# Attention in front of two dense layers: first pairs of heads without DRAM, chunks split at 128, K's high part on ScalarE

## The chip, the cores and the metric

The kernel runs on one core of a Trainium2 chip. The metric is the device time of one execution in microseconds; lower is better. The core has a matrix engine (TensorE, PE in the profile, with its weight loads as a row of their own, PEld), VectorE (DVE), ScalarE (ACT), GpSimd (POOL) and a sync engine (SP) from whose queue all DMA transfers are issued here. Every engine works through its own instructions in the order in which they stand in the program.

## What is computed

Attention over 4 batches of 8 heads, 576 positions of 64 values, with a bias from running sums of `s`, and then two dense layers with a nonlinearity each:

```python
def _attn_ref(q, k, v, s):
    scale = 1.0 / np.sqrt(D)
    scores = scale * np.matmul(q, k.transpose(0, 1, 3, 2))
    causal = np.triu(np.ones((S, S), dtype=bool), k=1)
    s_pos = np.maximum(s, 0.0)
    cum = np.cumsum(s_pos, axis=-1)
    bias = -(cum[:, :, :, None] - cum[:, :, None, :])
    scores = np.where(causal, -1000000000.0, scores + np.minimum(bias, 0.0))
    scores = scores - np.max(scores, axis=-1, keepdims=True)
    attn = np.exp(scores)
    attn = attn / (np.sum(attn, axis=-1, keepdims=True) + 1e-09)
    return np.matmul(attn, v)
x = attn_out.transpose(0, 2, 1, 3).reshape(2304, 512)
h = x @ w_in;  x = (h - np.tanh(h)) @ w_out
h = x @ w_in2; x = (h * np.clip(h + 3.0, 0.0, 6.0) / 6.0) @ w_out2
```

## The kernel before

A planner, `Plan`, holds every step with its engine, a duration, its predecessors and buffers and a priority (`PRIO`), and fixes the order on each engine before the program is built. All products of the attention but the last one, and of the dense layers, take numbers split into a high part that TensorE's faster float format holds exactly and a low part.

The 32 heads are worked on in 16 pairs (`heads(p)`). Of a pair, q and k come in transposed (64 rows by 2 x 576, tile `tq`). Four copies are made of them: Q high and K high (`q1` on ACT, `kh` on DVE) in the tiles Q and K of `firsts` (four sets), and in the tiles of `seconds` (two sets) once more Q high (`q2`, a DMA from tile to tile) and K high (`k2`, on ACT) with the low parts (`ql`, `kl`: subtractions on POOL). Rows 64 to 67 of Q and K carry the bias: two rows of K hold the running sums, as high and low part, and two rows of Q the negated maxima.

The running sums are made once, on DVE, at the start (L369 to L374, function `cum`): clipping, a scan, two copies. They go to DRAM (`cdram`) and from there into K by one DMA for each pair; for the first head they go from tile to tile by DMA (L256, K<-rb).

Softmax needs the row maxima before the scores. For each head PE makes the scores a first time from the high parts (L479, lists `MAXT`: five row blocks of up to 128 rows take 384, 576, 512, 256 and 128 columns, in one tile `wide` of two banks and two single banks), and DVE takes each block's maximum under the causal mask (L488), straight from the banks. The maxima of a pair are split and turned on DVE (L513 to L517), written to DRAM (`mo`, mdram) and read back as rows of Q (`mi`, Q<-mdram).

Then come the scores proper, transposed, in four chunks of columns (L572, lists `CHUNKS`): for each chunk one product from `seconds`, one from `firsts`, and one with `maskT` and the identity that adds the causal mask. The weights of these products are blocks of 128 columns of K. ACT takes the exponential (L575) and PE multiplies with v (L603) in plain float32, two passes for each product, into two banks that split the 576 queries at 256; ACT copies the two banks out (L626). Sums and results go on by DMA.

From about 200 us on the two dense layers follow on PE (L828, L859, then L1120, L1196); their weights are split on ACT and DVE during the attention and after. In the planner's rules PE steps that follow each other have a latency of 0.30 us between them.

## Time and profile before

| what | value |
|---|---|
| time, median of 3 runs | 969.19 us (969.17 to 972.99) |
| the profiled execution's own time | 968.87 us |
| its span, first to last instruction | 967.1 us |
| PE busy | 946.1 us (98%) |
| PE busy from 50 to 300 us | 249.5 us of 250 |
| DVE, ACT, POOL busy | 670.0, 467.9, 160.7 us |
| chain that ended last | PE 94%, DVE 3%, ACT 1%, DMA 1% |

How to read it: busy time is the time in which an engine had an instruction running. Matmuls are pipelined, so one matmul's listed duration overlaps the next one's, and a stretch in which PE is busy throughout can still hold fewer matmuls than another one: the number of matmuls in a window tells more than the busy share. Weight loads (PEld) run beside the matmul in front of them. The profiled execution is 0.3 us from the median.

### The profile page before, as it was taken

What the parts mean: (1) busy time and instruction counts of PE and PEld (TensorE: products, weight loads), DVE (VectorE), ACT (ScalarE), POOL (GpSimd) and SP (SyncE); (2) the same over time, 40 slices, a digit from 0 to 9 for tenths busy, and PEclk for the clock granted to TensorE, in tenths of its full rate; (3) what the DMA queues carried; (4) which work ended last, traced back from release to release, by engine and by line L of the source; (5) the groups of instructions that cost most, each with busy time, mean ns of one, the idle gap of its engine ahead of it and who ended that gap; (6) DMA issues with size and microseconds to landing.
All of it is one profiled execution on the core that took longest, in us unless ns stands there. A gap on an engine that the chain in (4) does not pass through costs nothing.

```text
span 967.1 us, 14956 instructions
## 1 busy us (share of the span) xinstructions
PE 946.1 (98%) x5560; PEld 838.7 (87%) x5560; DVE 670.0 (69%) x1107; ACT 467.9 (48%) x714; POOL 160.7 (17%) x106
## 2 busy tenths in 40 slices
PE   3999999999999999999999999999999999999998
PEld 3777777778878888998888888999999999999998
DVE  7887777759998667767766835555775567765763
ACT  2677667755444433444443433444454434544442
POOL 8344646520000000003322223000000000000000
PEclk9999999999999999999999999999999999999999
DMA  4656776676635356556455690765696657866562
GB/s 123 183 164 175 214 184 196 166 237 261 188 94 191 151 217 224 176 180 226 160 209 186 213 316 31 256 218 201 241 324 220 235 201 248 317 219 235 201 225 98
DMA packets 70521, 195.91 MB, mean 203 GB/s; under 512 B 11634, under 2 KB 20338, under 8 KB 69168
## 3 DMA queue, kind: packets, MB, share of 16 engines
q1 hardware_dynamic: 70448, 194.95, 61.3%
q8 instruction: 44, 0.72, 0.3%
q14 instruction: 29, 0.24, 0.1%
HBM read 143.75 MB, written 44.09 MB: 194 GB/s over the span
## 4 chain that ended last, share of the span: by engine, by line
PE 94%; DVE 3%; ACT 1%; DMA 1%; issue 0%; SPq 0%; DVEq 0%; ACTq 0%
PE bank L828 20%; PE bank L859 20%; PE pair L1196 19%; PE pair L1120 18%; PE bank L603 9%; PE bank L572 6%; PE wide L479 1%; DVE junk L488 1%; PE bank L479 1%; DMA Q<-mdram 0%; ACT w L776 0%; DVE f_w L1140 0%; DMA K<-rb 0%; SPq L440 0%; DVE rb L370 0%
## 5 line engine op out<-in xcount | busy, mean ns | idle before, releaser
L859 PE MATMUL bank<-gg,w 128*128 128x512 f32 (+1 forms) x960 | 234.3, 368 | 0.5 <-ACT gg L847 0.3
L828 PE MATMUL bank<-xx,w 128*128 128x512 f32 (+1 forms) x960 | 233.3, 368 | 0.0
L859 PEld LDWEIGHTS bank<-gg,w 128*128 128x128 f32 x960 | 170.1, 189 | 30.9 <-ACT gg L847 1.3
L828 PEld LDWEIGHTS bank<-xx,w 128*128 128x128 f32 x960 | 170.5, 188 | 30.3
L1120 PE MATMUL pair<-op_w,w 128*128 128x384 f32 x648 | 118.0, 334 | 0.6 <-DVE f_w L1140 0.6
L839 ACT ACTIVATE g<-bank 128x512 f32<-128x512 f32 (+1 forms) x80 | 44.5, 556 | 147.4 <-PE bank L828 124.2
L1196 PE MATMUL pair<-w,op_W 128*128 128x256 f32 x918 | 115.1, 283 | 0.0
L1120 PEld LDWEIGHTS pair<-op_w,w 128*128 128x128 f32 x648 | 112.5, 188 | 1.2 <-DVE f_w L1140 0.9
L603 PE MATMUL bank<-pt,vf 128*66 128x320 f32 (+4 forms) x448 | 112.6, 365 | 0.3 <-ACT pt L575 0.3
L1196 PEld LDWEIGHTS pair<-w,op_W 128*128 128x128 f32 x918 | 112.8, 192 | 0.0
L849 POOL TENSOR_TENSOR gg<-g,gg 128x512 fp32r<-128x512 f32 x32 | 47.5, 1484 | 345.0 <-ACT gg L847 307.9
L843 DVE TENSOR_TENSOR g<-bank,g 128x512 f32<-128x512 f32 (+1 forms) x80 | 50.9, 636 | 64.7 <-ACT g L839 64.0
L572 PE MATMUL bank<-Q,K 128*128 128x320 f32 (+9 forms) x384 | 94.2, 367 | 0.2 <-DMA Q<-mdram 0.2
L575 ACT ACTIVATE pt<-bank 128x512 f32<-128x512 f32 (+2 forms) x128 | 63.4, 501 | 43.4 <-PE bank L572 41.3
L572 PEld LDWEIGHTS bank<-Q,K 128*128 128x128 f32 (+1 forms) x384 | 65.3, 195 | 19.2 <-DMA Q<-mdram 0.6
L847 ACT ACTIVATE gg<-g 128x512 fp32r<-128x512 f32 (+1 forms) x80 | 47.0, 587 | 43.4 <-DVE g L843 35.0
L488 DVE CUSTOM_DVE_ANT_0 junk<-bank,maskA 128x512 bf16<-128x512 f32 (+2 forms) x96 | 45.0, 469 | 29.0 <-PE bank L479 21.6
L603 PEld LDWEIGHTS bank<-pt,vf 128*66 128x66 f32 (+1 forms) x448 | 51.8, 139 | 11.7 <-issue 1.6
L425 POOL TENSOR_TENSOR Q<-tq,Q 64x1152 fp32r<-64x1152 f32 (+1 forms) x17 | 42.4, 2494 | 60.1 <-PE bank L572 18.9
L488 DVE CUSTOM_DVE_ANT_0 junk<-wide,maskA 128x384 bf16<-128x384 f32 x64 | 41.8, 653 | 9.2 <-PE wide L479 4.6
L435 POOL TENSOR_TENSOR K<-tq,K 64x1152 fp32r<-64x1152 f32 (+1 forms) x17 | 42.8, 2520 | 23.2 <-DVE K L428 7.6
L1196 PE MATMUL pair<-w,op_B 128*128 128x256 f32 x342 | 44.1, 283 | 0.0
(305 smaller groups left out, 1299.5 us busy)
## 6 DMA issues: line engine op xcount, KB each, us to landing
w<-wdram SPq DMA_DIRECT2D x149, 512.0 KB
wdram<-cv SPq DMA_DIRECT2D x56, 512.0 KB
raw_c<-in_w_dram SPq DMA_DIRECT2D x11, 1024.0 KB
raw_b<-in_w_dram SPq DMA_DIRECT2D x11, 1024.0 KB
raw_a<-in_w_dram SPq DMA_DIRECT2D x12, 512.0 KB
...
```

Of the source, the lines that this page charges most:

```text
L488: nc.vector.tensor_tensor_reduce(out=junk[0:rr, 0:w], in0=r(b)[0:rr, col : col + w], in1=maskA[0:rr, m0 : m0 + w], scale=1.0, scalar=-3.0e ...
L572: nc.tensor.matmul(o, w, x, start=(i == 0), stop=(i == len(mms) - 1))
L575: nc.scalar.activation(r(pt), r(b)[:, 0 : CW[c]], AF.Exp, scale=0.125)
L603: nc.tensor.matmul(r(po[bank])[0:DV, oc : oc + n], r(vf)[0:rr, j, hh, :], r(pts[c])[0:rr, col : col + n], start=(j == 0), stop=(bank == 0 ...
L828: nc.tensor.matmul(r(ps)[:, 0:w], wt[:, c, :], x(c)[:, 0:w], start=(part == 0 and c == 0), stop=(part == 2 and c == NCC - 1),)
L839: nc.scalar.activation(r(g)[:, 0:w], r(ps)[:, 0:w], AF.Tanh)
L843: nc.vector.tensor_sub(x, r(ps)[:, 0:w], x)
L847: gho = plan.op("ACT", vec_us(w, 1.2, 205), lambda: nc.scalar.activation(r(gh)[:, 0:w], r(g)[:, 0:w], AF.Copy), [m, to_gg], [g, gh], base)
L849: glo = plan.op("DVE" if beside else "POOL", vec_us(w, 0.96, 155) if beside else vec_us(w, 0.44, 160), lambda: (nc.vector if beside else n ...
L859: nc.tensor.matmul(r(acc[e])[:, 0:w], a[:, es], bb[:, 0:w], start=f, stop=l)
L1120: nc.tensor.matmul(bank(k)[:, l], w[hw][:, l, kc], r(x)[:, hx, kc], start=(i in (1, 5, 2) and j == 0 and kc == 0), stop=(j == 2 and kc == ...
L1196: nc.tensor.matmul(r(c[k])[:, m * 256 : (m + 1) * 256], r(x)[:, hx, l, m * P : (m + 1) * P], w[hw][:, l], start=(i == order[chain_first[k] ...
```

## The change

1. The running sums at the start. Clipping moves to ACT (`relu`). The first head's high row is copied by DVE straight into K (`crow`); the second head's high row and both low rows come by DMA from tile to tile (`cu0_hi`, `cu0_lo`). The first pair's maxima use 65 rows, without the low row.
2. The maxima of the pairs 0 and 1 (`TURN`) no longer go through DRAM. DVE splits them into a tile `turn` (two steps a head, two instructions each), PE multiplies them with an identity (`identr`, weights of 4 columns, 128 moving columns, 20 such products), and ACT copies the result into rows 64 to 67 of Q (`put`). The rows for the first 256 queries go ahead of the rest, and the first score chunk waits for these alone.
3. From pair 2 on, the maxima of both heads are made together (`both`, `PAIRT`): the last 64 rows of the two heads share one block of 128 rows, so DVE takes nine maxima for a pair and not ten. PE makes that block in two pieces: 128 rows of head 1 from row 448 on, then the lower 64 rows anew from head 0.
4. `kh` moves from DVE to ACT. `k2` becomes a DMA from tile to tile for pairs 1 to 15, and stays on ACT for pair 0.
5. `CHUNKS` and the banks of the product with v split at 128 and not at 256: chunks 0 and 1 have 128 and 448 columns (before 256 and 320). A head's product with v has six products (before seven). The mask's product is the first of its chunk (before the last).
6. Eight products of the mask tile with itself (`WARM`) stand at PE's start. The rows of ones for the tiles of pairs 1 to 3 are written by POOL (pair 1) and ACT (pairs 2 and 3).
7. The planner's numbers: new `PRIO`, extra offsets for the first six pairs (`EARLY`), a DMA rate of 250 and not 220 KB/us, no latency between PE steps, at least 0.216 us for a float32 product.

On PE, the start. Before, the last maxima of pair 1 (L479, tiles K_1 and Q_1) in front of the first scores (L572, of pair 0):

```order
L479 MATMUL bank_65<-K_1_99,Q_1_98 128x512
L479 MATMUL bank_66<-K_1_99,Q_1_98 128x256
L479 MATMUL bank_66<-K_1_99,Q_1_98 128x128
L479 MATMUL wide<-K_1_99,Q_1_98 128x384
L479 MATMUL wide<-K_1_99,Q_1_98 64x128
L479 MATMUL wide<-K_1_99,Q_1_98 64x448
L572 MATMUL bank_70<-Q_0_104,K_0_105 128x256
```

Now, from the second head's maxima on (L644 are maxima, L566 the turning products, L709 scores):

```order
L644 MATMUL bank_71<-K_0_97,Q_0_96 128x128
L644 MATMUL bank_72<-K_0_97,Q_0_96 128x512
L566 MATMUL bank_73<-identr,turn 4x128 x2
L644 MATMUL wide<-K_0_97,Q_0_96 128x384
L644 MATMUL wide<-K_0_97,Q_0_96 64x128
L644 MATMUL wide<-K_0_97,Q_0_96 64x448
L709 LDWEIGHTS identb
L709 MATMUL bank_65<-maskT,identb 128x128
L709 MATMUL bank_65<-Q_0_104,K_0_105 128x128
L709 MATMUL bank_65<-Q_0_96,K_0_97 128x128
L566 MATMUL bank_66<-identr,turn 4x128 x3
```

Ahead of the first scores there stand the maxima of two heads and not of four, and one turning product.

On PE, a head's score chunks 0 and 1 in the running attention. Before:

```order
L572 MATMUL bank_70<-Q_0_104,K_0_105 128x256
L572 MATMUL bank_70<-Q_0_96,K_0_97 128x256
L572 LDWEIGHTS identb
L572 MATMUL bank_70<-maskT,identb 128x128
L572 MATMUL bank_65<-Q_0_104,K_0_105 128x320
L572 MATMUL bank_65<-Q_0_96,K_0_97 128x320
```

Now, for the same kind of place:

```order
L709 LDWEIGHTS identb
L709 MATMUL bank_71<-maskT,identb 128x128
L709 MATMUL bank_71<-Q_1_106,K_1_107 128x128
L709 MATMUL bank_71<-Q_1_98,K_1_99 128x128
L709 MATMUL bank_65<-Q_1_106,K_1_107 128x448
L709 MATMUL bank_65<-Q_1_98,K_1_99 128x448
```

The 256 and 320 columns have become 128 and 448, and mask and first product of chunk 0 are three matmuls of 128 columns with weights of 128 columns each.

On PE, the maxima that end in the tile `wide`. Before, one head's three matmuls are the rows `wide<-K,Q` of 384, 64x128 and 64x448 that stand in the first list; now, for a pair:

```order
L605 MATMUL wide<-K_2_101,Q_2_100 128x384
L605 MATMUL wide<-K_2_101,Q_2_100 128x128
L605 MATMUL wide<-K_2_101,Q_2_100 128x448
L605 MATMUL wide<-K_2_101,Q_2_100 64x128
L605 MATMUL wide<-K_2_101,Q_2_100 64x448
```

Two matmuls with weights of 128 columns (128 and 448 moving columns) stand between the 384 and the two of head 0's last 64 rows.

On ACT, the start. Before:

```order
L419 ACTIVATE Q_0_96<-tq 64x576
L431 ACTIVATE K_0_105<-tq 64x576
L419 ACTIVATE Q_0_96<-tq 64x576
L431 ACTIVATE K_0_105<-tq 64x576
L419 ACTIVATE Q_1_98<-tq 64x2x576
L431 ACTIVATE K_1_107<-tq 64x2x576
L575 ACTIVATE pt_0_111<-bank_70 128x256
```

Now:

```order
L358 ACTIVATE Q_3_102<-maskA 4x640 x2
L408 ACTIVATE rb<-rb 32x576
L358 ACTIVATE K_3_103<-maskA 4x576 x2
L472 ACTIVATE Q_0_96<-tq 64x576
L481 ACTIVATE K_0_97<-tq 64x576
L484 ACTIVATE K_0_105<-tq 64x576
L472 ACTIVATE Q_0_96<-tq 64x576
L481 ACTIVATE K_0_97<-tq 64x576
L484 ACTIVATE K_0_105<-tq 64x576
L358 ACTIVATE Q_2_100<-maskA 4x640 x2
L569 ACTIVATE Q_0_96<-bank_73 4x256
L358 ACTIVATE K_2_101<-maskA 4x576 x2
```

In front of the first head's maxima (`Q_0_96<-bank_73`, the first `put`) there now stand three rows of ones, the clipping, and K's high part twice for each head.

The core of the diff:

```diff
+TURN = (0, 1)
+WARM = 8
...
+SQ = 128
 CHUNKS = [
-    [(0, 0, 256, 0)],
-    [(0, 256, 320, 0)],
+    [(0, 0, SQ, 0)],
+    [(0, SQ, S - SQ, 0)],
     [(4, 512, 64, 0), (1, 128, 448, 64)],
     [(3, 384, 192, 0), (2, 256, 320, 192)],
 ]
-CW = [256, 320, 512, 512]
+CW = [SQ, S - SQ, 512, 512]
...
+PAIRT = [
+    [(0, 2, 384, 0), (2, 4, S, 384)], [(0, 3, 512, 0)], [(0, 1, 256, 0), (0, 0, 128, 256), (1, 0, 128, 384)],
+    [(1, 3, 512, 0)], [(1, 2, 384, 0)], [(1, 1, 256, 0)],
+]
...
-    DMA_US, DMA_KB_US, ISSUE = 1.6, 220.0, 0.55
+    DMA_US, DMA_KB_US, ISSUE = 1.6, 250.0, 0.55
...
-                        n.ready = max(n.ready, o.end)
+                        n.ready = max(n.ready, free["PE"] if o.eng == n.eng == "PE" else o.end)
...
+    sa = plan.op("ACT", 0.65, lambda: nc.scalar.activation(s_t, s_t, AF.Relu, scale=8.0), [ls], prio=lead - 30, name="relu")
+    cm = plan.op("DVE", 1.4, lambda: nc.vector.tensor_tensor_scan(
+        out=c_t, data0=c_t, data1=s_t, initial=0.0, op0=ALU.mult, op1=ALU.add), [sa, pk0], prio=lead - 29, name="cum")
+    cr = plan.op("DVE", 0.46, lambda: nc.vector.tensor_copy(c_row(0, 0), c_t[0:1]), [cm], prio=lead - 28, name="crow")
+    ch = plan.op("DVE", 0.46, lambda: nc.vector.tensor_copy(cp[0], c_t), [cm], prio=lead - 27, name="cumh", port=True)
+    cl = plan.op("DVE", 0.77, lambda: nc.vector.tensor_sub(cp[1], c_t, f32(cp[0])), [ch], prio=lead - 26, name="cuml")
+    cu0 = plan.dma(lambda: move(c_row(1, 0), cp[0][1:2]), 5, [ch, pk0], prio=lead - 25, name="cu0_hi")
+    cu1 = [plan.dma(lambda hh=hh: move(c_row(hh, 1), cp[1][hh : hh + 1]), 5, [cl, pk0], prio=lead - 24 + hh, name=f"cu0_lo{hh}") for hh in range(2)]
...
+    def warm():
+        for _ in range(WARM):
+            nc.tensor.matmul(r(wb)[:, 0:512], maskA[:, 0:P], maskA[:, 0:512], start=True, stop=True)
+
+    plan.op("PE", WARM * 0.427, warm, [pma], [wb], prio=lead - 50, name="warm")
...
-                return nc.vector.tensor_copy(r(b1)[1][0:64, a, 0:S], r(tq)[64:128, a])
+                nc.scalar.activation(r(b1)[1][0:64, a, 0:S], r(tq)[64:128, a], AF.Copy)
 
             def k2(a=a):
                 nc.scalar.activation(r(b2)[1][64:128, a, 0:S], r(tq)[64:128, a], AF.Copy)
+
+            def k2d(a=a):
+                move(r(b2)[1][64:128, a, 0:S], r(b1)[1][0:64, a, 0:S])
...
+            okh.append(plan.op("ACT", act, kh, [lk, al], [b1, tq], t + PRIO["kh"] + shift("kh") if p else lead - 0.95 + 0.3 * i + shift("kh"), name=f"kh{p}"))
+            if p:
+                ok2.append(plan.dma(k2d, 147 * n, [okh[-1], a2], [b1, b2], t + PRIO["k2"] + shift("k2"), name=f"k2_{p}"))
+            else:
+                ok2.append(plan.op("ACT", act, k2, [lk, a2], [b2, tq], lead - 0.9 + 0.3 * i + shift("k2"), name=f"k2_{p}"))
...
+                def split():
+                    m = r(mt)[:, hh, i0:i1]
+                    nc.vector.tensor_scalar_mul(slot[:, i0:i1, 2], m, -1.0)
+                    return nc.vector.scalar_tensor_tensor(
...
+                def rows():
+                    for i in range(i0, i1):
+                        nc.tensor.matmul(r(b)[0:4, (i - i0) * P : (i - i0 + 1) * P], slot[:, i], identr, start=(i == i0), stop=(i == i1 - 1), skip_group_check=True)
+
+                def put():
+                    nc.scalar.activation(r(b1)[0][64:68, hh, q0:q1], r(b)[0:4, 0 : q1 - q0], AF.Copy)
+
+                dep = [mm_mx[hh][c] for c in ((2,), (0, 1))[g]]
+                o = plan.op("DVE", 0.38, split, dep, [mt], u, name=f"mf{p}")
+                first_mf.append(o)
+                t = plan.op("PE", 0.08 * (i1 - i0), rows, [o, pid], [b], u, name=f"tr{p}")
+                return plan.op("ACT", vec_us(q1 - q0, 1.2, 200), put, [t, *(mm_pe[hh] if g else mm_pe[hh][2:])], [b, b1], u, name=f"mi{p}")
...
+                def mx(tiles=tiles, b=b):
+                    for hh, i, w, col in tiles:
+                        cut = 512 - col if col < 512 < col + w else w
+                        for h, q0, n_q in ((hh, i * P, P),) if hh < 2 else ((1, 448, P), (0, 512, D)):
+                            qa, ka = (t[:, h] for t in r(b1))
+                            for k0, n in ((0, cut), (cut, w - cut)):
+                                if n:
+                                    nc.tensor.matmul(
+                                        r(b)[0:n_q, col + k0 : col + k0 + n], qa[0:66, q0 : q0 + n_q], ka[0:66, k0 : k0 + n],
...
+                def rd(tiles=tiles, b=b):
+                    for hh, i, w, col in tiles:
+                        m = maskB if hh == 2 else maskA[:, 512 - i * P : 512 - i * P + w]
+                        nc.vector.tensor_tensor_reduce(
+                            out=junk[:, 0:w], in0=r(b)[:, col : col + w], in1=m,
...
+            low = [oq2[x], ok2[x], oql[x], okl[x], pmt] + (cu1 if p == 0 else [])
+            deps = [low + omi[hh][:1]] + [low + omi[hh]] * 3
...
+            if MASKS[c]:
+                mms.insert(0, mms.pop())
             for i, (o, w, x) in enumerate(mms):
-                nc.tensor.matmul(o, w, x, start=(i == 0), stop=(i == len(mms) - 1))
+                nc.tensor.matmul(o, w, x, start=(i == 0), stop=(i >= len(mms) - len(segs)), skip_group_check=True)
...
+                if q0 < SQ:
+                    n0 = min(SQ - q0, n)
...
-            q0, n = ((0, 256), (256, 320))[bank]
+            q0, n = ((0, SQ), (SQ, S - SQ))[bank]
...
+        ov0 = plan.op("ACT", 0.30, lambda: ov(0), [pvs[0]], [po[0]] + own, t0 + PRIO["ov"], name=f"ov{h}_0")
+        ov1 = plan.op("ACT", 0.55, lambda: ov(1), [pvs[3], ov0], [po[1]] + own, t0 + PRIO["ov"], name=f"ov{h}_1")
```

## Rows read from the trace of the kernel before

**Rows 1.** The page, part 1: busy us (share of the span) and instructions by engine.

```profile
PE 946.1 (98%) x5560; PEld 838.7 (87%) x5560; DVE 670.0 (69%) x1107; ACT 467.9 (48%) x714; POOL 160.7 (17%) x106
```

**Rows 2.** Waits of PE: what it waited for, total us, times, longest.

```profile
PE wide L479 <- DMA K<-rb: 9.9, 1, 9.9
PE wide L479 <- DVE MT L513: 3.3, 1, 3.3
```

**Rows 3.** Windows, PE: stretch, length, busy (matmuls), granted clock, DMA share, GB/s.

```profile
0.00:10.00 10.00, 0.07 (x1) 1.00 0.39 104
10.00:20.00 10.00, 6.62 (x21) 1.00 0.43 101
20.00:30.00 10.00, 8.63 (x37) 1.00 0.39 98
30.00:40.00 10.00, 9.77 (x58) 1.00 1.00 297
40.00:50.00 10.00, 9.59 (x57) 1.00 0.70 162
50.00:75.00 25.00, 25.00 (x152) 1.00 0.56 160
```

**Rows 4.** Timeline of the start: start, us, engine, line, operation.

```profile
4.07 0.68 ACT L419 ACTIVATE Q<-tq 64x576 fp32r<-64x576 f32 x1 [2.05 <-DMA tq<-in_q_dram]
...
5.39 1.35 DVE L370 TENSOR_TENSOR_SCAN rb<-rb 32x576 f32<-32x576 f32 x1
...
9.93 1.14 PE L479 MATMUL wide<-K,Q 66*128 66x384 f32 x3 [9.93 <-DMA K<-rb]
...
11.22 0.56 DVE L488 CUSTOM_DVE_ANT_0 junk<-wide,maskA 128x384 bf16<-128x384 f32 x1 [2.37 <-PE wide L479]
...
12.73 0.69 DVE L488 CUSTOM_DVE_ANT_0 junk<-bank,maskA 128x512 bf16<-128x512 f32 x1
...
13.57 0.42 DVE L488 CUSTOM_DVE_ANT_0 junk<-bank,maskA 128x256 bf16<-128x256 f32 x1
...
14.37 0.72 DVE L513 TENSOR_SCALAR MT<-Mt 128x5 fp32r<-128x5 f32 x1
...
15.56 0.40 SPq L256 DMA_DIRECT2D mdram<-mrow  x1
...
18.16 0.73 SPq L256 DMA_DIRECT2D Q<-mdram  x1
...
22.39 0.63 PE L572 MATMUL bank<-Q,K 128*128 128x256 f32 x2
```

**Rows 5.** Timeline, PE: the same three matmuls for two heads.

```profile
21.42 1.17 PE L479 MATMUL wide<-K,Q 66*128 66x384 f32 x3 [1.37 <-DVE Mt L488]
...
27.52 0.84 PE L479 MATMUL wide<-K,Q 66*128 66x384 f32 x3
```

**Rows 6.** Weight loads by shape, 50 to 190 us: busy us, mean ns.

```profile
L603 PEld LDWEIGHTS bank<-pt,vf 128*66 128x66 f32 x289 | 33.8, 138 | 4.4
...
L572 PEld LDWEIGHTS bank<-Q,K 128*128 128x128 f32 x149 | 27.0, 191 | 11.7
...
L572 PEld LDWEIGHTS <-identb 128*128 128x128 bf16 x74 | 7.2, 97 | 5.8
```

**Rows 7.** Timeline at 103 us, one score chunk: 64, 448, 64, 448 columns, and loads.

```profile
103.35 0.19 PEld L572 LDWEIGHTS bank<-Q,K 128*128 128x128 f32 x1
...
103.46 0.19 PEld L572 LDWEIGHTS bank<-Q,K 68*128 68x128 f32 x1
...
103.35 0.47 PE L572 MATMUL bank<-Q,K 128*128 128x64 f32 x2
...
103.66 0.48 PE L572 MATMUL bank<-Q,K 68*128 68x64 f32 x2
```

**Rows 8.** Window of the first dense layer, PE: length, busy (matmuls).

```profile
210.00:270.00 60.00, 60.00 (x267) 1.00 0.64 218
```

**Rows 9.** The page, part 5: one subtraction on POOL; busy us, mean ns, idle before.

```profile
L435 POOL TENSOR_TENSOR K<-tq,K 64x1152 fp32r<-64x1152 f32 (+1 forms) x17 | 42.8, 2520 | 23.2 <-DVE K L428 7.6
```

253 lines of the change are left out of this document (154 added, 99 removed), and 3 rows, old and new, of the table PRIO.

## Prediction

> **What bounds the kernel now.** I read the page's busy times first: PE is busy for 98% of the span [rows 1], so a change is worth what it takes from PE's work or from the time in which PE has none. Then I read what PE waited for: two waits of 9.9 and 3.3 us, both before the first scores [rows 2]. Then the windows, by the number of matmuls and not by busy time [rows 3]. From 50 to 75 us PE gets through 152 matmuls in 25 us, 164.5 ns each. The profile lists 35 matmuls for a head (6 for the maxima, 12 scores and 3 masks, 7 products with v in two passes), so a head takes 5.8 us. The five windows up to 50 us hold 1 + 21 + 37 + 58 + 57 = 174 matmuls, worth 174 x 0.1645 = 28.6 us. So 50 - 28.6 = **21.4 us are lost before 50 us**, and hardly any after. That is all that a better start can give; anything that lengthens a head's 5.8 us counts 32 times.
>
> Where the 21.4 us go is in the timeline. The first maxima start at 9.93 us, when the running sums have arrived in K by DMA. DVE is through with the first head's maxima at 14.37 us, the turned rows leave for DRAM at 15.56 us, the way back is issued at 18.16 us, and the first scores stand at 22.39 us [rows 4]. On top of the waiting, PE runs at half speed there: the same three matmuls take 1.17 us at 21.42 us and 0.84 us at 27.52 us [rows 5]. Their columns pass at 1.2 GHz in the first and at 2.4 GHz in the second case; the granted clock reads 1.00 in all windows [rows 3], so I go by the matmuls. In between PE had worked for 6.1 us without a gap.
>
> **The start, step by step.** ACT's order decides. The ones for pair 3's Q run while the inputs are on their way. The clipping on 32x576 is priced as the copy of 64x576, 0.68 us, and starts when `s` is there, about when q is, 4.07 us [rows 4]: done at 4.8 us. DVE's scan of 1.35 us [rows 4] ends at 6.2 us and the short copy into K at about 6.7 us. ACT meanwhile writes the ones for pair 3's K (two pieces of 0.68 us, to 6.15 us), then Q high and K high of the first head, to 7.5 us. So the first maxima start at about **7.6 us** (before: 9.93).
>
> DVE then works through the two heads. From the start times of its five maxima [rows 4] the blocks of 384 and 576 together take 1.51 us, 512 takes 0.84, 256 and 128 together 0.80. The order is now 256 and 128 first, 512, split, 384 and 576; then the second head. DVE's first block is there at 8.4 us: 384 columns at 1.2 GHz are 0.32 us, and from 9.93 to 11.22 us it took 0.49 us beyond the 0.8 us of 960 columns. For a split, two small instructions, I take 0.38 us; three of that kind take 1.19 us from 14.37 to 15.56 us, so 0.79 us is the most. First head: 9.2, 10.0, 10.4 (rows for 256 queries ready), 11.9 us; second head's 256 and 128 at 12.7 us, the two splits that are due at 13.5 us, the rest with its split at 16.2 us. ACT has six copies and the ones for pair 2's Q ahead of the first `put` (6 x 0.68 us from 6.15 us: 10.25 us; ones: 11.75 us), so the first rows of Q are there at 12.15 us, the ones for pair 2's K hold ACT to 13.5 us, the first exponential is out at 13.8 us, the second `put` at 14.25 us. From about **14.3 us** on PE always has scores or products with v at hand, up to the second pair's maxima. By then it has done 12 + 3 + 2 = 17 matmuls that also the kernel before has, 2.8 us: 11.5 us are lost.
>
> What is lost after that: PE is at half speed until it has worked on for a while. As 6.1 us did it before, I take 6.1 us again, of which half is lost, 3.0 us. For waits from then to 50 us I take 1.6 us: the windows from 30 to 50 us lost 20 - 115 x 0.1645 = 1.1 us [rows 3], and now the maxima of two more heads stand in that stretch, with DVE behind them. Sum 11.5 + 3.0 + 1.6 = 16.1 us, a **gain of 21.4 - 16.1 = 5.3 us**. Bounds: the clock up at once and no later wait, 9.9 us gained; twice the time at half speed, 2.3 us gained.
>
> **What is added to PE's work.** The columns stay the same in number, but short matmuls do not hide their weight loads. At 103 us the loads for 64 and 448 columns start 0.11 us apart, and from one 64 to the next, over 64 + 448 = 512 columns, it is 0.31 us [rows 7]. In the dense layer a matmul of 512 columns takes 60 / 267 = 0.225 us at most [rows 8]. So a load of 128 weight columns takes 0.11 us, and a matmul shorter than that makes the next one wait. By shape the loads confirm it: 191 ns for 128 weight columns, 138 ns for 66 [rows 6], of which a part is latency that passes beside others. A matmul of 128 columns alone takes 128 / 2.4 = 53 ns, so it leaves some 57 ns open if 128 weight columns follow.
> - Scores: mask and first product of chunk 0 are now such matmuls, 2 x 57 ns. Before, 256 and 320 columns hid every load there, but the mask, last, stood before one at times. I take 0.10 us a head. The mask of chunk 2 (192 columns, 80 ns) now stands before a load: 0.02 us.
> - Products with v: one matmul fewer, equal columns, 66 weight columns: between 0 and -0.06 us; I take -0.02.
> - Maxima of 14 pairs: two more matmuls of 128 columns before 128 weight columns: 0.11 us a pair, 1.6 us.
> - Turning products: 20 of 128 columns behind weights of 4, at 0.06 us: 1.2 us.
>
> Together 32 x 0.10 + 1.6 + 1.2 = **6.0 us more**. Bounds: +0.6 us if no load shows (turning products less the products with v saved), +7.5 us if each place costs its full 57 ns.
>
> The Trainium skill, page "TensorE: Matmul & The Clock Gate", section "LDWEIGHTS (loading the stationary operand)", gives a weight load a time by its columns alone, number of columns / 1.2 in ns: an estimate of 107 ns for 128. The trace agrees with its 0.11 us between two loads. By the page the open part is 54 and not 57 ns, and the sum 0.3 us less. It is a rule that speaks against splitting at 128.
>
> **What costs nothing as long as it is covered.** DVE loses a reduction and K's copy in each pair and gets a copy of one column; it is not waited for from 50 us on, so the relief is worth nothing. ACT gives up one copy of at most 2 x 0.68 us a pair and takes another. The 15 new DMAs for K stand in SP's queue, and POOL's subtraction for K's low part (2.5 us each [rows 9]) now waits for one. The cover is the other pair's 11.6 us of PE work. The dense layers keep their matmuls; only the order of two kinds of steps changes there, which costs nothing where PE has both at hand.
>
> **Sum.** 968.9 us (the profiled execution's own time) + 6.0 - 5.3 = 969.6 us; the median lies 0.3 us above that execution: **969.9 us**, no change that can be told. A measurement of this kernel can tell about 0.5% from no change, 4.85 us: faster is below 964.3, slower above 974.0.
>
> **Rivals.**
> A: the whole start comes. The eight matmuls at PE's start keep it at 2.4 GHz for the first maxima and scores, and no wait follows. For it: they cost nothing, since PE has no other work before 7.6 us and they take 8 x 512 / 1.2 = 3.4 us. Against it: PE was busy for 6.6 of the 10 us before 20 us [rows 3] and still slow at 21.42 us [rows 5], and here gaps follow until 14.3 us. Price: 9.9 us gained and not 5.3: 965.3 us.
> B: the loads do not show, since they are drawn forward behind longer matmuls. Against it: [rows 7] shows them in the middle of the running attention. Price: +0.6 and not +6.0: 964.5 us; with A 959.9 us.
> C, on the other side: K's high part comes too late in the running attention. Before, ACT wrote it to `seconds` in at most 1.4 us; a DMA from tile to tile with its issue takes about what the maxima's way to DRAM takes, 2.6 us from 15.56 to 18.16 us [rows 4], behind whatever SP's queue holds. `seconds` has two sets, so a pair's copy (2.6 us) and two subtractions (5.0 us) must fit between the last scores of the pair before last and its own first scores, one pair's 11.6 us. 4 us are left. If SP's queue holds the copy longer, because it stands behind DMAs that themselves wait, PE waits. Behind two of 2.6 us it is 5.2 us late, 1.2 us over; in 5 of 14 pairs that is 6 us: 975.9 us. For it: SP issues everything in one order, and 15 more are in it. Against it: no PE wait from 50 us on today.
>
> **How the numbers follow.** Forecast 0.52 (all of it within 0.5%), A 0.13 (some of it with parts of B: 0.05 faster, 0.08 within), B 0.10 (faster), C 0.25 (slower). Faster 0.15, same 0.60, slower 0.25. The range takes in the bounds: low 962.5 us (A with half of B), high 977.0 us (C, or 7.5 us of work with 2.3 us of gain and a few waits).
>
> **What would show it.** First maxima at 7.6 us, first scores at about 12.5 us, PE without idle from 14.3 us. In windows from 50 to 190 us the head takes about 5.9 and not 5.8 us. A chunk 0 whose three matmuls start 0.11 us apart shows the loads. Waits of PE for Q or K rows from DMA, or for POOL, after 50 us would show C. I am wrong if the attention's end has moved forward by over 4 us, or if PE idles in the running attention.

## The result, and the profile of the changed kernel

The changed kernel takes **982.1 us** (median of 6 runs, 979.9 to 984.5), the kernel before 969.3 in the same rounds: a ratio of **1.0125, 95% interval 1.0104 to 1.0146**. The forecast was 969.9, and its range ended at 977.0. The profiled execution took 979.9 us with a span of 978.1 us, against 967.1 us before: 11.0 us to explain. (A few executions, one each of x6, x9 and the kernel before and two of x11, took 1047.6 to 3315.4 us; every median and comparison here leaves them out.)

PE stays the bound. The page, part 1, answers [rows 1]; the windows of PE answer [rows 3]. The columns are the same as there; the last four rows are from a second answer with finer windows.

```profile
PE 964.3 (99%) x5524; PEld 828.2 (85%) x5524; DVE 651.2 (67%) x1082; ACT 473.3 (48%) x733; POOL 156.9 (16%) x108
```

```profile
0.00:10.00 10.00, 6.84 (x17) 1.00 0.40 117
10.00:20.00 10.00, 8.00 (x34) 1.00 0.67 163
20.00:30.00 10.00, 9.54 (x39) 1.00 0.62 136
30.00:40.00 10.00, 7.79 (x40) 0.85 0.71 189
40.00:50.00 10.00, 10.00 (x40) 0.64 0.56 150
50.00:75.00 25.00, 25.00 (x140) 1.00 0.63 162
75.00:100.00 25.00, 25.00 (x139) 1.00 0.75 193
...
100.00:125.00 25.00, 25.00 (x140) 1.00 0.91 216
125.00:150.00 25.00, 25.00 (x137) 1.00 0.88 234
150.00:175.00 25.00, 24.27 (x132) 1.00 0.92 219
175.00:200.00 25.00, 24.58 (x136) 1.00 0.67 170
```

A head is now 33 records (6 maxima, 15 scores and masks, 12 products with v). From 50 to 100 us it takes 33 x 50 / 279 = 5.914 us, before 35 x 25 / 152 = 5.757 us. Counted by matmuls as in the prediction, one record is worth 25 / 139.5 = 0.179 us. Of the 90 records up to 30 us, 8 are the warming matmuls and 10 turning products, so 72 belong to heads; from 30 to 50 us it is 80 less 10 turning products. That gives the time that PE did not spend on heads ("lost"):

| stretch | before | forecast | after |
|---|---|---|---|
| 0 to 30 us | 30 - 59 x 0.1645 = 20.3 | 14.5 | 30 - 72 x 0.179 = 17.1 |
| 30 to 50 us | 1.1 | 1.6 | 20 - 70 x 0.179 = **7.5** |
| 50 to 200 us, beyond a head's own time | 0.5 (605 of 608 records from 100 us on) | 0 | 2.3 (545 of 558) |
| 32 heads, longer by | - | 6.0 - 1.2 = 4.8 | 32 x 0.157 = 5.0 |

The start came, 3.2 us by 30 us; all of it and 3.2 us more are gone again by 50 us. In the window from 40 to 50 us PE is busy without a gap and gets 40 matmuls done where a window of 25 us at full clock holds 140: the granted clock is 0.64 there. It is 0.50, the lower of its two levels (1.2 GHz), from 38 to 46 us:

```profile
36.00:38.00 2.00, 1.63 (x11) 0.76 0.98 259
38.00:46.00 8.00, 7.94 (x26) 0.50 0.93 246
```

What came ahead of the fall are waits of PE. They stand in the list of its waits from 25 to 52 us (what it waited for, total us, times, longest) and in the timeline (start, us, engine, line, operation):

```profile
PE wide L644 <- DVE Mt L653: 1.0, 1, 1.0
PE wide L605 <- DVE Mt L653: 0.7, 1, 0.7
PE bank L566 <- DVE turn L560: 0.5, 1, 0.5
...
```

```profile
27.27 0.17 DVE L559 TENSOR_SCALAR turn<-Mt 128x2 fp32r<-128x2 f32 x1
27.34 2.61 POOL L478 TENSOR_TENSOR Q<-tq,Q 64x1152 fp32r<-64x1152 f32 x1 [6.77 <-ACT Q L472]
27.47 2.50 DVE L560 SCALAR_TENSOR_TENSOR turn<-Mt,turn 128x2 fp32r<-128x2 f32 x1
29.89 0.54 DVE L653 CUSTOM_DVE_ANT_0 junk<-wide,maskA 128x384 bf16<-128x384 f32 x1
30.02 0.28 PE L566 MATMUL bank<-identr,turn 128*4 128x128 f32 x2 [0.48 <-DVE turn L560]
...
31.29 0.44 PE L644 MATMUL wide<-K,Q 66*128 66x384 f32 x1 [0.98 <-DVE Mt L653]
```

Line 560 is the second instruction of a split, on 128 x 2 values. It takes 2.50 us and ends when POOL's subtraction ends; in the other seven splits of this kernel it takes 0.16 or 0.17. Behind it wait the maxima of four heads (two pairs stand one behind the other there), and behind these PE.

At the end of the attention the loss is 12.5 us: the first matmul of the dense layers starts at 209.43 us before and at 221.91 us now (line 828, now 965). The dense layers then lose 1.5 us less than before.

```profile
209.43 7.68 PE L828 MATMUL bank<-xx,w 128*128 128x512 f32 x32
```

```profile
221.91 4.27 PE L965 MATMUL bank<-xx,w 128*128 128x512 f32 x17
```

### The profile page after: what moved, and what is told of

It reads as the page before. It is cut to its first block, busy times and chain, and to the rows that moved or that the text cites. A ratio compares the mean times of both kernels' runs of the same rounds, so it can differ in the third digit from the quotient of the medians.

```text
span 978.1 us, 14833 instructions
## 1 busy us (share of the span) xinstructions
PE 964.3 (99%) x5524; PEld 828.2 (85%) x5524; DVE 651.2 (67%) x1082; ACT 473.3 (48%) x733; POOL 156.9 (16%) x108
## 4 chain that ended last, share of the span: by engine, by line
PE 94%; DVE 2%; DMA 2%; ACT 1%; issue 0%; SPq 0%; DVEq 0%; ACTq 0%
PE bank L996 20%; PE bank L965 20%; PE pair L1333 19%; PE pair L1257 18%; PE bank L740 8%; PE bank L709 6%; PE bank L605 1%; PE wide L605 1%; DVE junk L653 1%; DMA tq<-in_k_dram 1%; DMA K<-cdram 1%; DMA tq<-in_q_dram 1%; DVE turn L559 0%; DVE junk L613 0%; DVE turn L560 0%
## 5 line engine op out<-in xcount | busy, mean ns | idle before, releaser
L996 PE MATMUL bank<-gg,w 128*128 128x512 f32 (+1 forms) x960 | 210.5, 368 | 0.3 <-ACT gg L984 0.3
L965 PE MATMUL bank<-xx,w 128*128 128x512 f32 (+1 forms) x960 | 210.4, 368 | 0.0
L1257 PE MATMUL pair<-op_w,w 128*128 128x384 f32 x612 | 111.8, 334 | 0.0
L740 PE MATMUL bank<-pt,vf 128*66 128x448 f32 (+4 forms) x384 | 108.0, 406 | 0.0
L1257 PEld LDWEIGHTS pair<-op_w,w 128*128 128x128 f32 x612 | 106.5, 188 | 0.1
L709 PE MATMUL bank<-Q,K 68*128 68x448 f32 (+9 forms) x384 | 85.1, 351 | 0.2 <-DMA tq<-in_k_dram 0.2
L740 PEld LDWEIGHTS bank<-pt,vf 128*66 128x66 f32 (+1 forms) x384 | 45.9, 140 | 30.9 <-issue 19.3
L709 PEld LDWEIGHTS bank<-Q,K 68*128 68x128 f32 (+1 forms) x384 | 61.2, 204 | 10.0 <-issue 7.4
L613 DVE CUSTOM_DVE_ANT_0 junk<-bank,maskA 128x512 bf16<-128x512 f32 (+3 forms) x98 | 47.1, 480 | 31.4 <-PE bank L605 22.2
L1333 PEld LDWEIGHTS pair<-w,op_B 128*128 128x128 f32 x342 | 42.4, 192 | 0.0
```

What stands on the lines that cost most here:

```text
L613: nc.vector.tensor_tensor_reduce(out=junk[:, 0:w], in0=r(b)[:, col : col + w], in1=m, scale=1.0, scalar=-3.0e38, op0=ALU.add, op1=ALU.max, ...
L709: nc.tensor.matmul(o, w, x, start=(i == 0), stop=(i >= len(mms) - len(segs)), skip_group_check=True)
L740: nc.tensor.matmul(r(po[bank])[0:DV, oc : oc + n], r(vf)[0:rr, j, hh, :], r(pts[c])[0:rr, col : col + n], start=(j == 0), stop=(j == (0, 2 ...
L965: nc.tensor.matmul(r(ps)[:, 0:w], wt[:, c, :], x(c)[:, 0:w], start=(part == 0 and c == 0), stop=(part == 2 and c == NCC - 1),)
L996: nc.tensor.matmul(r(acc[e])[:, 0:w], a[:, es], bb[:, 0:w], start=f, stop=l)
L1257: nc.tensor.matmul(bank(k)[:, l], w[hw][:, l, kc], r(x)[:, hx, kc], start=(i in (1, 5, 2) and j == 0 and kc == 0), stop=(j == 2 and kc == ...
```

## The experiments

Theory H: DVE's splits, held by POOL's subtractions, delay the maxima of pairs 1 and 2, and the half clock doubles the price. Rivals: R, DVE is too slow for four heads' maxima in a row in any case; C, rows come too late by DMA; W, the added work of PE is larger than counted. "Lost" below is read from the windows as above.

### x1_pool_order: another order of POOL's subtractions

```diff
-oql.append(plan.op("POOL", pool, ql, [oq1[-1], a2] + (first_mf[: p == 1] if p else [ch]), [b1, b2, tq],
+oql.append(plan.op("POOL", pool, ql, [oq1[-1], a2] + (first_mf[: p == 1] + first_mf[7:8] * (p == 2) if p else [ch]), [b1, b2, tq],
...
-okl.append(plan.op("POOL", pool, kl, [ok2[-1]], [b2, tq],
+okl.append(plan.op("POOL", pool, kl, [ok2[-1]] + first_mf[7:8] * (p == 2), [b2, tq],
```

> Only POOL's order changes: pair 2's subtraction for Q's low part (2.61 us at 27.34 us in the changed kernel's trace) starts after pair 1's last split instead of beside its first one, and pair 1's own subtraction for K goes ahead of it. Theory H (the held split is the cause): the split's second instruction takes 0.16 us and not 2.50, DVE's maxima of pairs 1 and 2 come 2.3 us earlier, PE's waits between 29.5 and 38 us go, the granted clock stays at 1.00 from 36 to 48 us, and PE has 4 to 5 us less lost by 50 us: 976 to 979 us against 982.1. Rival R (the maxima of four heads stand one behind another and DVE is the slower of the two there): the waits shift but stay, the clock falls to 0.50 all the same, and the time is 980.5 to 982.5 us.

Measured: 980.5 us, ratio 1.0108 (1.0088 to 1.0128). The hold did not go. It has only changed its partner, as the timeline shows: pair 1's own subtraction for K, which now stands ahead, starts at 26.27 us and holds the split's first instruction for 2.61 us.

```profile
26.27 2.62 POOL L491 TENSOR_TENSOR K<-tq,K 64x1152 fp32r<-64x1152 f32 x1 [5.69 <-PE bank L644]
26.30 2.61 DVE L559 TENSOR_SCALAR turn<-Mt 128x2 fp32r<-128x2 f32 x1
```

The run does not tell H and R apart. It shows that the planner's edges only set an order; they make nobody wait.

### x5_pool_late: the same for pair 1's subtraction, by an edge only

```diff
-rd_done.extend(rds)
+rd_done.extend(rds); [(o.next.append(okl[0]), setattr(okl[0], "left", okl[0].left + 1)) for o in first_mf[6:7] if p == 1]
```

> The run with POOL's order changed did not take the hold away: pair 1's subtraction for K's low part, now ahead, started at 26.27 us when K's high part had landed by DMA, and held the split's first instruction for 2.61 us (26.30 us). Here that subtraction waits for pair 1's third split and pair 2's for Q for its fourth, so no subtraction can run beside the first three; up to 45 us the other engines' orders are those of the changed kernel. Theory H: the splits take 0.17 us each, DVE's chain from 27 us on is 2.5 us shorter, PE idles under 1.5 us between 25 and 40 us (changed kernel: 2.7 us in the four windows), and if that is what lets the clock fall, it stays at 1.00 from 30 to 50 us: 975 to 978.5 us. Rival R (DVE's rate on four heads' maxima): PE still idles 2 us and more there and the clock falls again: 980 to 983 us.

Measured: 981.4 us (1.0117; 1.0082 to 1.0153), a miss for the same reason: the subtraction started at 25.85 us with its data, and the splits were held for 1.38 and 1.63 us.

### x9_no_hold: POOL really waits

```diff
     for o in plan.schedule():
         ins = o.fn()
+        if o.name == "mf1":
+            last_split = ins
+        if o.name in ("kl1", "ql2", "kl2"):
+            tc.add_manual_dep(
+                ins.ins, last_split.ins.name,
+                mybir.DependencyInfo(mybir.DependencyClass.Sync, mybir.DependencyReason.DATA), reason="turns",
+            )
```

(with the edges of the two kernels above.)

> In the last run of this kind nothing made POOL wait, so pair 1's subtraction still started with its data at 25.85 us and DVE's splits were held for 1.38 and 1.63 us. Here that subtraction really waits for pair 1's third split, pair 2's two for the fourth (a wait on DVE's count). PE's and DVE's orders are the changed kernel's up to 45 us. Theory H: every split of pair 1 takes under 0.2 us an instruction, DVE's chain is 2.5 to 3 us shorter, PE idles under 1.5 us between 25 and 40 us, the granted clock does not fall there: 975 to 978.5 us. Rival R (DVE's rate on the four heads' maxima that stand there together, about 3 us a head): PE still idles 2 us or more and the clock falls: 980 us and more. A third result, less idle time and the clock falling all the same, would mean that the fall does not hang on these 2.5 us.

Measured: 977.1, 977.9 and 974.4 us, ratio **1.0064** (1.0040 to 1.0089): 5 to 6 us of the 12.8 are back. The splits take 0.16 to 0.17 us, POOL's subtraction starts at 29.95 us:

```profile
26.75 0.17 DVE L559 TENSOR_SCALAR turn<-Mt 128x2 fp32r<-128x2 f32 x1
...
29.95 2.64 POOL L491 TENSOR_TENSOR K<-tq,K 64x1152 fp32r<-64x1152 f32 x1 [9.36 <-DVE turn L560]
```

```profile
25.00:40.00 15.00, 14.20 (x83) 1.00 0.72 190
36.00:48.00 12.00, 11.24 (x61) 1.00 0.82 205
112.00:118.00 6.00, 4.07 (x26) 0.99 0.83 220
118.00:124.00 6.00, 6.00 (x18) 0.50 0.95 234
```

From 25 to 40 us PE idles 0.8 us (changed kernel: 2.7, sum of its windows), does 83 matmuls (65 there), and the clock does not fall. That is H: only POOL's three subtractions were made to wait, and the orders of PE and DVE are the same up to 45 us (ACT's up to 36 us, that of the DMA issues up to 32 us; from there the new plan differs). R is out as the main cause.

The last two rows show the same price a second time, further on: 1.93 us of idle time behind one row of K, then 6 us at half the clock, which cost some 3 us.

```profile
107.93 0.25 SPq L266 DMA_DIRECT2D K<-cdram  x1
...
117.09 1.10 PE L605 MATMUL wide<-K,Q 66*128 66x384 f32 x5 [1.93 <-DMA K<-cdram]
```

A DMA of 9 KB, issued at 107.93 us, lets PE go on at 117.09 us. That is rival C's place. In the changed kernel's own profile PE waits only 0.6 us for that row; in that of x2, which differs only in the mask's place, 1.9 us in two waits.

### x13_k_copy_cut: K's copies with an eighth of the bytes

```diff
-move(r(b2)[1][64:128, a, 0:S], r(b1)[1][0:64, a, 0:S])
+move(r(b2)[1][64:128, a, 0 : S if p == 1 else 72], r(b1)[1][0:64, a, 0 : S if p == 1 else 72])
```

> The version without the hold, and from the third pair on the DMA that copies K's high part from tile to tile moves 72 of 576 columns; the rest of the copy is left out, so later scores are made with a K that is partly an older pair's. Order, waits and number of DMAs are the same; only the bytes (288 KB each, 14 times) are gone. Theory Q (these bytes fill the queues and make the rows for the maxima land late): DMA share from 100 to 150 us falls from 0.82 to about 0.72, the wait of 1.9 us at 115 us for the running sums' row in K goes, the granted clock does not fall at 118 us, and 5 to 7 us come back: 970.5 to 973 us. Rival P (the row's place in SP's queue and the buffers decide): the wait stays within 0.5 us, 976 to 978 us.

Measured: **972.1 us** (1.0024; 1.0008 to 1.0040), 5 us below the version it is made from (4 us by the ratios). The wait for the running sums' row is gone; the only one left between 60 and 250 us is 0.7 us for POOL. The window from 100 to 150 us, first without the hold (x9), then with the small copies:

```profile
100.00:150.00 50.00, 48.07 (x241) 0.93 0.82 206
```

```profile
100.00:150.00 50.00, 49.34 (x272) 1.00 0.80 202
```

Theory Q holds on x9: the bytes of the copies, at an unchanged order, make rows late. It was not tried on the changed kernel itself. The kernel before had DMA shares of 0.65, 0.74 and 0.68 from 50 us on in windows of 50 us, the changed one 0.69, 0.90 and 0.80. The DMA share from 100 to 150 us fell less than I had expected (0.80, not 0.72). In this profiled execution the clock fell once more, at 35 to 45 us, after 0.8 us of idle time; in x9, with as much, it did not. The runs (970.7 to 977.4 us) spread accordingly.

### x10_filled: matmuls of no use in two gaps at 30 us

```diff
 def rows():
+    more = p == 1 and (hh, g) == (0, 0)
+    for _ in range(4 * more):
+        nc.tensor.matmul(r(b)[:, 0:512], maskA[:, 0:P], maskA[:, 0:512], start=True, stop=True)
     for i in range(i0, i1):
...
+    for _ in range(9 * more):
+        nc.tensor.matmul(r(b)[:, 256:512], maskA[:, 0:P], maskA[:, 0:256], start=True, stop=True)
```

> The changed kernel with 13 matmuls of no use in PE's two longest gaps of the stretch (4 of 512 columns before the first turning product of pair 1 at 30 us, 9 of 256 behind it, 1.9 us in all at 2.4 GHz); they write a bank that is then overwritten or not read. The waits themselves stay. Theory G (the clock falls because PE stands still too much between 25 and 38 us; the fall costs 4.8 us, the waits 4 us): the granted clock stays at 1.00, or falls for a shorter time, and the time is 2 to 5 us shorter, 977 to 980 us. Rival (the clock falls for another reason, or the gaps from 35 to 38 us suffice): it falls as before, and the time is 982 to 984 us.

Measured: 982.9 us (1.0127; 1.0078 to 1.0176), a miss. PE was busy for 4.97 and 4.74 of 5 us up to 35 us, but from 35 to 40 us it idled 1.0 us at the next waits, and the fall came there, a little later and longer (0.50 from 40 to 50 us):

```profile
35.00:40.00 5.00, 4.02 (x20) 0.74 0.90 211
```

Filling one gap moves the fall to the next. Whether gaps decide these later falls stays open, also by x9 and x13; x16 below tests it at the start.

### x4_k_high_back: K's high part by DVE again from pair 1 on

```diff
 def kh(a=a):
+    if p:
+        return nc.vector.tensor_copy(r(b1)[1][0:64, a, 0:S], r(tq)[64:128, a])
     nc.scalar.activation(r(b1)[1][0:64, a, 0:S], r(tq)[64:128, a], AF.Copy)
...
-ok2.append(plan.dma(k2d, 147 * n, [okh[-1], a2], [b1, b2], t + PRIO["k2"] + shift("k2"), name=f"k2_{p}"))
+ok2.append(plan.op("ACT", act, k2, [lk, a2], [b2, tq], t + PRIO["k2"] + shift("k2"), name=f"k2_{p}"))
```

> From the second pair on DVE makes K's high part and ACT its second copy again, so the 15 DMAs from tile to tile are gone; the order is planned anew. My rival C (the DMA brings K's high part late, or its place in SP's queue holds others up): PE's waits between 150 and 200 us (0.6, 0.4, 0.2 us) go, and 2 to 3 us of the time with them: 979 to 980 us, unless DVE, which gets 15 copies back, delays the maxima between 25 and 50 us by more. Rival (the late waits come from elsewhere, since the rows that they wait for are the running sums' and the inputs', not K's high part): waits of the same size stay, 981 to 983 us.

Measured: 987.3 us (1.0171; 1.0145 to 1.0196), worse. Up to 50 us it is better: the granted clock stays at 1.00 from 25 to 48 us. But the new plan leaves DVE with too much later on; PE waits for K from DVE 2.3 us, for the sums' row 1.2 us, for the maxima's rows 1.0 us between 60 and 250 us. My rival C, read as "K's high part itself comes late", is not what this shows; that the copies' bytes hurt had to wait for x13.

### x2_mask_last, x3_split_256, x6_before_128: the parts of PE's added work

x2, x3 (both on the changed kernel) and x6 (on the kernel before), in this order:

```diff
-                mms.insert(0, mms.pop())
+                pass
...
```

```diff
-SQ = 128
+SQ = 256
...
```

```diff
-    [(0, 0, 256, 0)],
-    [(0, 256, 320, 0)],
+    [(0, 0, 128, 0)],
+    [(0, 128, 448, 0)],
...
```

> Only the place of the mask's matmul in a score chunk changes: last, as in the kernel before, and not first; no other engine's order moves. My prediction put 0.02 us a head on the mask of chunk 2 and counted the mask of chunk 0 with the split, so it expects 981.0 to 982.1 us. If a mask in front makes the weight load behind it wait in every one of its three chunks (96 masks, up to 0.05 us each), mask last gives 977.5 to 980 us.

> The queries of a head are cut at 256 again and not at 128, everything else as changed; the order of the steps is planned anew with it. My prediction has 0.08 to 0.10 us a head on the cut (32 heads, 2.6 to 3.2 us): 50 to 150 us hold 1.4% more heads, and 978.9 to 979.5 us come out if the stretch before 50 us is no better. Rival (the loads do not show): no change in the heads per stretch, 981.5 to 982.5 us. The first scores need the first 256 queries in both versions, so the start itself should not move; what moves between 25 and 50 us is the new plan's and is read from the windows.

> The kernel before with one part of the change alone: a head's queries cut at 128 and not at 256 (chunks of 128 and 448 columns), the mask last as it was; the order is planned anew with the same rules. My prediction's term for this is 0.08 to 0.10 us a head, minus 0.02 for one product with v less: 32 heads make 2 to 3 us, 971.5 to 972.5 us. If the loads do not show: 968.5 to 970 us. The windows from 50 to 190 us give the time of a head directly.

Measured: mask last 979.4 us (1.0098; 1.0075 to 1.0120), 2.7 us below the changed kernel and inside the range of a mask that costs; but its four runs reach from 976.5 to 982.5, with the clock's falls. From 50 to 100 us it does 280 records, the changed kernel 279. At the attention's end, where both work without a gap, a head takes 5.11 us with the mask last (205.10 to 210.21 us) and 5.14 with it first (205.04 to 210.18). So a mask in front costs about 0.03 us a head there, an estimated 1 us for 32 heads; the rest of the 2.7 us is not explained.

Cut at 256 again: 981.7 us (1.0120; 1.0106 to 1.0134). The new plan lost in the start what it saved later (1.93 of 5 us busy from 30 to 35 us, clock 0.51 from 40 to 50 us), so this one says nothing on the cut.

The clean answer is the kernel before with the cut alone: **971.4 us, ratio 1.0017** (1.0007 to 1.0027), 1.6 us with an interval from 0.7 to 2.6, and no fall of the clock. Counting gives a head of 33 x 100 / 570 = 5.79 us (570 records from 50 to 150 us; before 5.757). The trace is more exact, since in both kernels the heads follow each other evenly. Here the first product with v of a head stands beside that of the head ten later, before and then with the cut:

```profile
94.32 0.60 PE L603 MATMUL bank<-pt,vf 128*66 128x256 f32 x2
...
152.66 0.60 PE L603 MATMUL bank<-pt,vf 128*66 128x256 f32 x2
```

```profile
95.48 0.39 PE L603 MATMUL bank<-pt,vf 128*66 128x128 f32 x2
...
154.54 0.38 PE L603 MATMUL bank<-pt,vf 128*66 128x128 f32 x2
```

That is 5.83 and 5.91 us a head: 0.07 us more, 2.3 us for 32 heads. I had 2 to 3 us for it, and the loads show. It also says how far counting can be off: 5.757 for 5.83 us.

### x7_old_running and x8_old_running_k: the start with the old running attention

x7 joins x2 and x3 and gives every head maxima of its own again; x8 adds x4's edit.

```diff
-        if p not in TURN:
-            rds = both()
-            maxima(0, slice(0, 2))
-        for hh in range(2) if p in TURN else ():
+        for hh in range(2):
...
-            maxima(hh, slice(hh, hh + 1))
+            if p in TURN:
+                maxima(hh, slice(hh, hh + 1))
+            elif hh:
+                maxima(0, slice(0, 2))
```

> The changed kernel's start with the running attention of before: cut at 256, mask last, every head's maxima of its own; K's high part stays with ACT and the DMA. PE's work is then that of before but for the turning products (1.2 us). Theory W (the added work is real and costs what PE does more): 5 to 6 us less work than the changed kernel, 975 to 977.5 us if the stretch from 25 to 50 us loses as much as there. If the stretch is what the new plan makes of it, the time differs by what it loses there, which the windows show; if nothing were lost there, 964 to 966 us.

> As the one before, and from the second pair on K's high part by DVE and its copy by ACT, so no DMA from tile to tile for K. In the changed kernel alone this took the loss between 25 and 60 us from 9.3 to 4.5 us (no fall of the granted clock there) and brought new waits for DVE between 75 and 250 us, where DVE has a copy and the head's own maxima more. Theory: the first gain stays, since K's low part no longer waits for a DMA: 5 us better than the kernel without it before 60 us, 970 to 973 us, if the waits after 75 us stay below 2 us; rival: DVE as the slower engine makes PE wait for K or maxima again and again, 978 us and more.

Measured: 980.5 us (1.0109; 1.0094 to 1.0124) and 988.9 us (1.0196; 1.0164 to 1.0227). The first has less work and is no faster, since its plan ran into three holds in a row (2.61, 2.59, 2.53 us; the last stands here); PE waited 6.4 us for two splits and then worked at half the clock:

```profile
33.11 2.53 DVE L559 SCALAR_TENSOR_TENSOR turn<-Mt,turn 128x3 fp32r<-128x3 f32 x1
```

```profile
35.00:50.00 15.00, 13.98 (x51) 0.50 0.60 161
```

The second kept the start's gain (from 25 to 50 us it does 145 matmuls at a granted clock of 1.00) and then lost more at DVE (3.1 us at once for K's high part, clock 0.76 from 175 to 225 us). Who takes over K's high part must have the time for it.

### x11, x12, x14, x15: the change without its detours

All four: cut at 256, mask last, K's second copy by ACT in every pair (so no K copies by DMA), and an order planned with PE at half speed up to 23.5 us and with splits held beside subtractions, the priorities searched anew. x11 and x14 have each head's own maxima, x12 the changed kernel's for two heads; x14 is planned with slower DMAs; x15 is x11 again, for a profile.

```diff
-                    free[e] = t + o.dur
+                    dur = o.dur * (2 if e == "PE" and t < 23.5 else 1)
+                    if e == "DVE" and o.name in ("mf0", "mf1") and port > t:
+                        dur = max(dur, port - t)
+                    free[e] = t + dur
```

and in x14 besides:

```diff
-    DMA_US, DMA_KB_US, ISSUE = 1.6, 250.0, 0.55
+    DMA_US, DMA_KB_US, ISSUE = 2.0, 200.0, 0.55
```

> A version that keeps the change's start and gives up what the runs showed to cost: cut at 256, mask last, maxima of each head of its own, K's second copy by ACT in every pair (no DMA from tile to tile for K), and an order planned with PE at half speed up to 23.5 us and with DVE's splits held while a subtraction runs. Theory (what the change lost is added work of PE, the stretch from 25 to 50 us and the late rows of K): about 17 us lost by 50 us against 22.9 in the kernel before, no waits of PE over 1 us from 50 to 200 us, no fall of the granted clock after 25 us, PE's work 1 to 2 us above before: 963 to 967 us. Rival (ACT, with 1.2 us more a pair, becomes what PE waits for): waits for ACT's copies and exponentials between 50 and 200 us, 968 us and more.

> As the one before, but with the changed kernel's maxima of two heads in one step from the third pair on, and with priorities of its own. My prediction has 0.11 us a pair on that in PE's work, 1.6 us in all, against which DVE has one reduction less a pair: 0.5 to 2 us above the version with each head's own maxima if the stretch to 50 us is as good, 965 to 969 us.

> The version without the detours (start of the change; cut at 256, mask last, each head's own maxima, K's second copy by ACT), planned anew with slower DMAs (200 KB a microsecond and 2.0 us for each, where the changed kernel counts with 250 and 1.6 and the one before with 220 and 1.6). If late rows are what is left to lose, this order waits for none after 50 us: PE loses 16 to 19 us by 50 us and 1 to 2 more by 200, 961 to 966 us. If ACT's extra copy a pair is what PE waits for, or the falls of the clock come back, 967 to 971 us.

> The same kernel as the first without detours, whose profiled execution ran at half speed from end to end and can't be read. A usable profile of it: lost by 50 us about 17 us; if it then has waits for rows from DMA between 60 and 200 us of 2 us and more, its 969.5 us are the start's gain given back there; if it has none, PE's work is more than counted. 967 to 970 us.

Measured: 968.8 us (0.9989; 0.9975 to 1.0003), 971.7 (1.0014; 0.9998 to 1.0029), 972.8 (1.0029; 1.0017 to 1.0040), 969.3. x11, x12 and x14 miss the times expected of them. The list of PE's waits of x15 names none between 18 and 250 us, and that of x14 none between 24 and 250 us, so the detours are gone and late rows are not what is left. What is left is the clock: 0.50 up to beyond 30 us, where the changed kernel works at full speed from about 23.8 us on (the same two matmuls of 448 columns take 1.10 us at 15.01 us, and 0.81 us at 23.82; the rows stand under "The start" below). Ahead of that PE has gaps. The longest, 1.8 us at 15.4 us, stands behind ACT, which makes two copies for the next pair ahead of the `put`:

```profile
15.00:20.00 5.00, 3.16 (x14) 0.50 0.49 121
...
25.00:30.00 5.00, 5.00 (x17) 0.50 1.00 246
30.00:35.00 5.00, 5.00 (x26) 0.80 0.15 25
```

```profile
15.74 1.16 ACT L487 ACTIVATE K<-tq 64x1152 fp32r<-64x1152 f32 x1
...
16.81 0.67 ACT L571 ACTIVATE Q<-bank 4x320 fp32r<-4x320 f32 x2
...
17.27 1.22 PE L711 MATMUL bank<-Q,K 68*128 68x320 f32 x3 [1.84 <-ACT Q L571]
```

x12 shows the other half: 25.00 of 25 us busy from 25 to 50 us, and afterwards 1.9 us of waiting for the sums' row, although it has no K copies; it gives back what it won.

### x16_filled_start: the version without detours, gaps filled

```diff
-WARM = 8
+WARM = 11
...
+                    for _ in range(2 if (p, hh, c) == (0, 1, 2) else 0):
+                        nc.tensor.matmul(r(b)[:, 0:512], maskA[:, 0:P], maskA[:, 0:512], start=True, stop=True)
...
+            for _ in range((2, 4)[c] if h == 0 and c < 2 else 0):
+                nc.tensor.matmul(ps[:, 0:512], maskA[:, 0:P], maskA[:, 0:512], start=True, stop=True)
```

The banks that they write are overwritten right behind.

> The version without detours (its readable profile: no wait after 18 us, but a granted clock of 0.50 up to 31 us, where the changed kernel's matmuls are fast from 23.5 us on) with 11 more matmuls of no use in PE's four gaps between 5 and 17 us: 3 behind the first eight, 2 ahead of the second head's first maxima, 2 and 4 ahead of the first two score chunks; the orders are the same. Theory G (PE comes to full speed the later, the more it stands still at the start): full speed from 20 to 25 us on instead of 31, which is worth 3 to 5 us: 964.5 to 966.5 us. Rival (the time to full speed does not hang on these gaps): full speed at 31 us again and 969 to 970 us, or a little more where the matmuls of no use delay one that matters.

Measured: **965.8 us, ratio 0.9975** (0.9954 to 0.9997) against the kernel before: the only version whose interval lies below 1. The orders are x15's; only matmuls of no use were added.

```profile
15.00:20.00 5.00, 4.36 (x24) 0.83 0.50 127
20.00:25.00 5.00, 4.35 (x28) 1.00 1.03 236
25.00:30.00 5.00, 4.37 (x24) 1.00 1.00 253
```

The granted clock is at 1.00 from 20 us on, where x15 gets there after 30 us, and PE does 52 matmuls from 20 to 30 us, where x15 does 38. By the medians 3.0 us of time come with it (expected: 3 to 5), by the profiled executions 4.5; three of the ten runs, 969.4 to 973.3 us, lack the gain, and the intervals of the two ratios overlap. PE has more idle time now, 1.3 us from 20 to 30 us. So in this pair of profiles the gaps at the start set when PE gets to full speed.

## Why the prediction was wrong, step by step

**Bound and method: right.** PE is busy for 99% of the span, and counting matmuls instead of busy time found the loss again.

**The start: right in its chain, too large by 2.6 us.** Forecast: first maxima at 7.6 us, the first `put` at 12.15, first scores at 12.5, PE in work from 14.3. Measured, against [rows 4]: 6.57, 10.88, 12.62 and 15.0 us.

```profile
6.57 1.23 PE L644 MATMUL bank<-K,Q 65*128 65x256 f32 x3 [1.55 <-ACT K L481]
...
8.94 1.19 DVE L559 TENSOR_SCALAR turn<-Mt 128x2 fp32r<-128x2 f32 x1
...
10.88 0.37 ACT L569 ACTIVATE Q<-bank 4x256 fp32r<-4x256 f32 x1 [0.29 <-PE bank L566]
...
15.01 1.10 PE L709 MATMUL bank<-Q,K 128*128 128x448 f32 x2
...
23.82 0.81 PE L709 MATMUL bank<-Q,K 128*128 128x448 f32 x2
```

Up to 30 us the gain was forecast at 20.3 - 14.5 = 5.8 us and is 3.2: PE is at half speed from 15.0 to some point before 23.8 us, where I had 6.1 us of it, and turning products and waits for splits stand in it.

**The step that failed: "For a split, two small instructions, I take 0.38 us" and "For waits from then to 50 us I take 1.6 us".** It is 7.5 us. The split was priced by its size, with an upper bound of 0.79 us from a row of three small instructions. That row held the warning: line 513 takes 0.72 us at 14.37 us [rows 4], where such an instruction alone takes 0.16 us. I took it for its own duration; it ends when a memset of POOL ends:

```profile
13.90 1.16 POOL L339 MEMSET Q<- 4x1280 f32 x1
```

With POOL at work a split lasts until POOL is done, up to 2.6 us (x1, x7), and it stands ahead of the next maxima. The waits themselves are the smaller part of the price: PE idles 2.2 us from 30 to 50 us, and the granted clocks of 0.85 and 0.64 in the two windows cost about 5 us (an estimate, 0.15 x 10 + 0.36 x 10). I had charged the half clock once, at the start, and not behind later waits. x9 gives 5 us back by holding three subtractions.

**PE's added work: near in sum.** Forecast 4.8 us for 32 heads and 1.2 us for turning, 6.0 us; by counting it is 5.0 for the heads. Of its parts the cut is near the forecast (2.3 us, x6), and a mask in front costs an estimated 1 us (x2) where I had 0.02 us a head for one mask and counted another with the cut. What two heads' maxima cost was not told apart: counting is good to about 0.07 us a head (x6), some 2 us in 32 heads.

**"What costs nothing as long as it is covered": wrong for the K copies.** The 15 DMAs of 288 KB hide behind PE's work as such, but they share the queues with the rows for the next maxima. My rival C had the slower direction and the place (rows from DMA after 50 us), but put the lateness in SP's order; x13 shows the bytes. Its price, 6 us, is near the 5 us that x13 gives back only by luck: I had summed five delays of 1.2 us, and x9 has one wait of 1.9 us with half a clock behind it.

**Where the 11.0 us of the profiled runs are:** 2.0 us up to 50 us (3.2 less 1.2 for the turning products, counted as work), 6.2 us of work, 1.8 us from 50 to 200 us, together 10.0 us. At the attention's end it is 12.5, and the dense layers return 1.5. The 2.5 us between 10.0 and 12.5 are not placed by counting, which takes all records alike: at 200 us the changed kernel has 64 of its 384 products with v still ahead, the kernel before 32 of 448, and the last 40 take 9.6 us (from 212.32 us on), 0.24 us each and not 0.179. So some of what is lost before 200 us does not show in the table.

**The range** took in C or a bad start, not both together. x9 and x13 return one after the other 5 and 5 us, but that the two add up in the changed kernel is not shown: x13 is built on x9, and in the profiled execution of the changed kernel PE waits 0.8 us for rows and inputs by DMA after 50 us, with no fall of the clock there. That the 972.1 us that then stand lie near the forecast of 969.9 does not confirm the forecast: x13 is another kernel and leaves out part of a copy.
